# Windowed attention with block summaries, then a hard-swish MLP: every engine's queue in the order of the program, attention cut into parts by engine

## The chip, the cores and the metric

The kernel runs on one core of one Trainium2 chip. A core has a matrix engine (TensorE, PE in the profile), three engines for element-wise work (VectorE or DVE, ScalarE or ACT, GpSimd or POOL) and SyncE (SP), which here only issues transfers. Each engine works through a queue of its own, in order, and waits at semaphores for the others. The metric is device time in microseconds (us); less is better.

## The reference

Attention over 4 batches, 8 heads, 768 positions of 64 columns; then a two-layer MLP on the 3072 rows of 512 columns that the heads give together.

```python
k_sum = k.reshape(B, H, nb, block, D).max(axis=3)      # block = 32, nb = 24
v_sum = v.reshape(B, H, nb, block, D).mean(axis=3)
scores_l = scale * (q @ k^T), kept where abs(i - j) < 16
scores_s = scale * (q @ k_sum^T) + log(block)
a = softmax(concat(scores_l, scores_s))
x = (a @ concat(v, v_sum)), heads side by side         # 3072 x 512
h = x @ w_in                                           # 512 x 2048
out = (h * clip(h + 3, 0, 6) / 6) @ w_out              # 2048 x 512
```

## The kernel before

**Attention.** Heads go in four pairs p per batch b. For a query block of 64 positions the kernel forms one column block of 128 key rows: 64 own keys, 24 block maxima (rows 64 to 87), 16 keys after the block and 16 before it (the *edges*). `kx[p]` holds these for all 12 blocks, `qx[p]` the queries of both heads, `va[b % 2]` the values in the same row order, with weights for the denominator. Steps, with their lines:

- `Tk` (L241): 16 PE transposes of k into a PSUM tile `tpk`; ACT copies it into `kx` (L250); DVE takes the block maxima (L258), spreads them (L261), and copies the two edges from `tpk` (L271, L272).
- `Tq` (L274): transposes of q into `tpq`; ACT copies one head's half, DVE the other (L294; L296 for batch 3).
- `Sc` (L298): score matmuls for up to four blocks (L308), ACT's exponential into `at` (L310). In batches 0 and 1 the mask is added on PE (L304), in 2 and 3 DVE multiplies by it (L312).
- `AV` (L316): values times weights into `num`, denominators into `den`; ACT takes logarithm and exponential for the reciprocal (`lg`), DVE multiplies into `x` (L352; L337, L338 for batches 2 and 3). `num` and `den` have one buffer each.
- `v` of batches 0 and 1 is loaded as float32 (`vf`), cast into `va` by DVE and GpSimd (`cast_v`, L117), its block sums come from PE (`sum_v`, L389) and go into `va` through DVE (L391) and GpSimd (`put_sums`, L395). For batches 2 and 3 GpSimd sets the weights (12 memsets, L485), loads v straight into `va` (L127) and adds rows (`vsum`, L142).

**MLP.** 768 rows of a batch make two tiles of 384 rows, 8 tiles in all. `F1(t, ft)` (L356): four matmuls of 128x384 (L362) into `hp`, ACT's relu `r` (L365), DVE's product `g` (L366). `F2(t, i)` (L368): one matmul of 128x512 (L374); after 16 of them ACT copies the result `ot` and SP stores it. `hp` has two buffers, four where no F2 runs beside F1. `g` tiles and the two `vf` tiles share a pool of three.

**Order.** The work list (L526) is F1(0), F2(0), F1(1), F2(1), F1(2), then F1(t) with F2(t-1) for t = 3 to 7, then F2(7); each entry has 16 steps, here called *slots*, numbered 16n + i. A dictionary `plan` puts attention calls behind slots. But the program's order binds only GpSimd throughout; for PE, ACT, DVE and SP it binds up to L445 alone:

```python
    ctx.enter_context(tc.manual_schedule(engines={ET.Pool}))
    start = tc.manual_schedule(engines={ET.PE, ET.Activation, ET.DVE, ET.SP})
    start.__enter__()
    ...
    start.__exit__(None, None, None)
```

From there a scheduler, working at build time, picks each of these four queues' order from what the plan emits. A load issued by GpSimd waits until the transfer eight before it has landed, as the built program has eight semaphores for them.

Of the kernel before, what the change touches and what calls it, by code (L numbers as in the profile page):

```python
# [15 lines left out]
D = 64  # L16
# [16 lines left out]
def kernel(  # L33
# [39 lines left out]
    kx = [const.tile([128, NQ, 128], BF16, tag=f"kx{p}", name=f"kx{p}") for p in range(NP)]  # L73

    qx = [const.tile([128, NQ, 2, QB], BF16, tag=f"qx{p}", name=f"qx{p}") for p in range(NP)]
# [33 lines left out]
    def load_vf(b, p):  # L109

        t = vf_t[b][:, 2 * p:2 * p + 2].rearrange("r h s d -> r (h s) d")
        nc.gpsimd.dma_start(out=t, in_=v[b, 2 * p:2 * p + 2].rearrange("h s d -> (h s) d").rearrange("(s r) d -> r s d", r=128))

    def cast_v(eng, b, p, odd, lo, hi):

        t = vf_t[b][64 * odd:64 * odd + 64, 2 * p:2 * p + 2, lo:hi]
        eng.tensor_copy(va[b % 2][0:QB, p, 2 * lo + odd:2 * hi:2, 0:3:2].rearrange("r t j d -> r j t d"), t)  # L117
# [42 lines left out]
    start = tc.manual_schedule(engines={ET.PE, ET.Activation, ET.DVE, ET.SP})  # L160
    start.__enter__()
# [22 lines left out]
    q0 = rows_tile(ld_tile("qb"), 8, RUN // 2)  # L184
    load("k", 0, 0, 1, t=(k0, 0))
# [3 lines left out]
    load("q", 0, 0, 1, 0, t=(q0, 0))  # L189
    load_vf(0, 0)  # L190
    load_vf(0, 1)
# [13 lines left out]


    nc.vector.memset(zero[:], 0.0)
    nc.vector.memset(half_c[:], 0.5)

    nc.vector.memset(ind[:], 0.0)  # L210
    for u in range(4):
        nc.vector.memset(ind[32 * u:32 * u + 32, 28 + u:29 + u], 1.0)

    def zero_kq(p):
        nc.vector.memset(words(kx[p][:, :, R_SUM + NB:R_NEXT]), 0.0)
        nc.vector.memset(words(kx[p][:, 0, R_PREV:]), 0.0)
        nc.vector.memset(words(kx[p][:, NQ - 1, R_NEXT:R_PREV]), 0.0)
        for j in range(2):
            nc.vector.memset(words(qx[p][64 * j:64 * j + 64, :, 1 - j]), 0.0)

    for p in range(3):
        zero_kq(p)

    def zero_rest():
        nc.vector.tensor_scalar(mask[:], maskb[:], 1.0 / BIG, 1.0, op0=ALU.mult, op1=ALU.add)
        zero_kq(3)
        nc.vector.memset(ones[:, 1], 0.0)
        for i in (0, 2):
            nc.vector.memset(ones[:, i], 1.0)
            nc.vector.memset(ones[R_SUM:R_NEXT, i], float(BLK))  # L230

    def zero_va(i, p):
        z = zero[:].unsqueeze(2)
        nc.scalar.copy(words(va[i][:, p, :, 1]), z.to_broadcast([128, NQ, D // 2]))
        o = va[i][R_NEXT:, p, 0:NQ:NQ - 1].rearrange("r t j d -> r t (j d)").bitcast(F32)
        nc.scalar.copy(o, z[R_NEXT:].to_broadcast([32, 2, 3 * D // 2]))

    for p in range(NP):
        zero_va(0, p)

    def Tk(b, p):  # L241
        pool, tag = (ps_o, "o") if b == 0 else (ps_s, "s")
        tp = pool.tile([128, S], BF16, tag=tag, name="tpk")
        t = kq_t["k", b, p, None]
        o = kx[p][:, :, 0:QB]
        if b < NLONG:
            for s in range(RUN):
                for j in range(2):
                    nc.tensor.transpose(tp[64 * j:64 * j + 64, s * RP:(s + 1) * RP], t[:, j, s], ident[0:RP, 0:RP])  # L249
            nc.scalar.copy(o.rearrange("p t (c s) -> p t c s", s=RUN),  # L250
                           tp[:].rearrange("p (s t c) -> p t c s", s=RUN, t=NQ))
        else:
            for s in range(NT):
                nc.tensor.transpose(tp[:, s * 128:(s + 1) * 128], t[:, s].rearrange("p h d -> p (h d)"), ident[:])
            nc.scalar.copy(o, tp[:].rearrange("p (t c) -> p t c", t=NQ))
        red = work.tile([128, NB], BF16, tag="red", name="red")
# [4 lines left out]
        nc.vector.tensor_copy(kx[p][:, :, R_SUM:R_SUM + NB], red[:].unsqueeze(1).to_broadcast([128, NQ, NB]))  # L261
        if b < NLONG:
            e = EDGE // RUN
            src = tp[:].rearrange("p (s t c) -> p t c s", s=RUN, t=NQ)
            tail, head = src[:, 0:NQ - 1, RUN - e:], src[:, 1:, 0:e]
            put = lambda o: o.rearrange("p t (c s) -> p t c s", s=RUN)
        else:
            src = tp[:].rearrange("p (t c) -> p t c", t=NQ)
            tail, head = src[:, 0:NQ - 1, QB - EDGE:], src[:, 1:, 0:EDGE]
            put = lambda o: o  # L270
        nc.vector.tensor_copy(put(kx[p][:, 1:, R_PREV:]), tail)  # L271
        nc.vector.tensor_copy(put(kx[p][:, 0:NQ - 1, R_NEXT:R_PREV]), head)  # L272

    def Tq(b, p, half=None):  # L274
        pool, tag = (ps_h, "h") if b == 0 else (ps_s, "s")
        tp = pool.tile([128, S], BF16, tag=tag, name="tpq")
        t = kq_t["q", b, p, half]
        r = RUN if half is None else RUN // 2
        n = r * RP
        t0 = 0 if half is None else half * NH  # L280
        nt = n // QB
        if b < NLONG:
            for s in range(r):
# [5 lines left out]
        for j in range(2):  # L289
            rows = slice(64 * j, 64 * j + 64)  # L290
            copy = nc.vector.tensor_copy if j else nc.scalar.copy
            o = qx[p][rows, t0:t0 + nt, j]
            if b < NLONG:
                copy(o.rearrange("p t (c s) -> p t c s", s=r), tp[rows, 0:n].rearrange("p (s t c) -> p t c s", s=r, t=nt))  # L294
            else:
                copy(o, tp[rows].rearrange("p (t c) -> p t c", t=NQ))  # L296

    def Sc(b, p, lo, hi):  # L298
# [7 lines left out]
        for i in range(n):  # L306
            t = lo + i
            nc.tensor.matmul(sp[:, i], kx[p][:, t], qx[p][:, t], start=not on_pe, stop=not on_pe or i == n - 1)  # L308
        a = at[p][:, lo:hi]
        nc.scalar.activation(a, sp[:, 0:n], AF.Exp, scale=scl)  # L310
        if not on_pe:
            nc.vector.tensor_tensor(a, a, mask[:, m0:m0 + n].unsqueeze(2).to_broadcast([128, n, 2, QB]), op=ALU.mult)  # L312

    xt = {}

    def AV(b, p, half):  # L316
# [3 lines left out]
        a = at[p]  # L320
        alt = b == 0 and half == 0 and p % 2 == 1
        pool = ps_o if alt else ps_n
        num = pool.tile([128, HALF], F32, tag="o" if alt else "num", name="num")
        den = pool.tile([128, HALF], F32, tag="o" if alt else "den", name="den")
        lg = work.tile([128, HALF], F32, tag="lg", name="lg")
        if b in DEN_IN_VALUES:

            for j, o in enumerate((num, den)):
                for i in range(NH):
                    t = half * NH + i  # L330
                    w = va[b % 2][:, p, t].rearrange("p j d -> p (j d)")
                    nc.tensor.matmul(o[:, i * QB:(i + 1) * QB], w[:, j * D:j * D + 128], a[:, t, j],
                                     start=True, stop=True)
            nc.scalar.activation(lg[0:64], num[64:128], AF.Ln)
            nc.scalar.activation(lg[64:128], den[0:64], AF.Ln)  # L335
            nc.scalar.activation(lg[:], lg[:], AF.Exp, scale=-1.0)
            nc.vector.tensor_tensor(xt[s][0:64, p], num[0:64], lg[0:64], op=ALU.mult)  # L337
            nc.vector.tensor_tensor(xt[s][64:128, p], den[64:128], lg[64:128], op=ALU.mult)  # L338
            return
        for i in range(NH):  # L340
            t = half * NH + i
            w = va[b % 2][:, p, t].rearrange("p j d -> p (j d)")
            for j in range(2):
                nc.tensor.matmul(num[:, i * QB:(i + 1) * QB], w[:, j * D:j * D + 128], a[:, t, j],
                                 start=(i == 0 and j == 0), stop=(i == NH - 1 and j == 1))
        w = ones[:].rearrange("p j d -> p (j d)")
        for j in range(2):
            nc.tensor.matmul(den[:].rearrange("p (t c) -> p t c", c=QB), w[:, j * D:j * D + 128],
                             a[:, half * NH:(half + 1) * NH, j], start=(j == 0), stop=(j == 1))
        nc.scalar.activation(lg[:], den[:], AF.Ln)  # L350
        nc.scalar.activation(lg[:], lg[:], AF.Exp, scale=-1.0)  # L351
        nc.vector.tensor_tensor(xt[s][:, p], num[:], lg[:], op=ALU.mult)  # L352
# [31 lines left out]
    vs0 = [const.tile([R_NEXT, 2, D], BF16, tag=f"vs0{p}", name="vs0") for p in range(NP)]  # L384

    def sum_v(b, p):
        sums = ps_n.tile([128, 2, D], F32, tag=("num", "den")[p % 2], name="sums")
# [3 lines left out]
        nc.vector.tensor_copy(vs0[p][R_SUM:], sums[R_SUM:R_NEXT])  # L391
# [5 lines left out]

    def S_first(p):
        Sc(0, p, 0, 4)
        Sc(0, p, 4, 6)  # L400

    k1 = rows_tile(ld_tile("kb"), 4, RUN)

    def load_pair(p):
        load("k", 0, p, 1, t=(k1, 2 * p - 4) if p > 1 else (k0, 2 * p))
        load("q", 0, p, 1, 0, t=(q0, 2 * p))

    def v_first(p):
# [3 lines left out]
    load_pair(1)  # L412
    Tk(0, 0)
    Tq(0, 0, 0)
    zero_rest()
    cast_v(nc.gpsimd, 0, 0, 0, 0, 4)
    S_first(0)
    v_first(0)
    sum_v(0, 0)
    load_vf(0, 2)  # L420
    load_pair(2)
    put_sums(0, 0, 0, NH)
# [145 lines left out]
```

## Time and profile before

| | |
|---|---|
| median of two timed runs | 294.39 us (293.48 and 295.3) |
| the profiled execution | 293.38 us, span 291.7 us |
| busy: PE, DVE, ACT, POOL | 240.7, 158.8, 176.4, 113.7 us |
| mean granted TensorE clock | 0.958 |
| read from and written to HBM | 30.4 and 6.3 MB |

PE's busy time by stage, from the windows of the trace:

| stretch (us) | what runs | PE busy | clock |
|---|---|---|---|
| 0 to 40 | batch 0, first half | 22.06 of 40 | 0.96 |
| 40 to 71.3 | F1 of tile 0 | 11.14 of 31.3 | 0.67 |
| 71.3 to 128 | F2(0), F1(1), F2(1); attention of batches 0 and 1 | 55.63 of 56.7 | 1.00 |
| 128 to 153.5 | F1(2); end of batch 1, start of batch 2 | 21.94 of 25.5 | 1.00 |
| 153.5 to 235.4 | F1 and F2 together; batches 2 and 3 | 77.85 of 81.9 | 1.00 |
| 235.4 to 291.7 | F1 and F2, no attention | 52.05 of 56.3 | 0.99 |

How to read the profile: a line of the page's second part gives an engine's busy share in 40 equal slices of the span, as digits. A line of waits is "engine line waited for: us in total, times, longest". A timeline line is start, duration, engine, line, operation, output and input with shapes, count, and in brackets the idle time before it and what ended that. A window's line gives for each engine busy us and, in brackets, instructions.

### The profile page before, as it was taken

The page shows a single profiled execution, that of the slowest core. Times are in us where ns is not written, and L with a number is a line of the kernel's source. Part 1 is how long each engine was busy: PE and PEld are TensorE (multiplying, and loading weights), DVE is VectorE, ACT ScalarE, POOL GpSimd, SP SyncE. Part 2 cuts the span into 40 slices and gives each one's busy share as a digit, 9 for nine tenths or more (in the row PEclk, how much of TensorE's full clock was granted, in tenths as well). Part 3 has the DMA queues.
Part 4 walks back from the last instruction along what each step waited for, and adds up shares of the span by engine and source line. Part 5 has one row for each costly group of instructions (what it writes and reads, how often), then busy time and mean ns, then how long its engine had stood idle before and what let it go on. Part 6 is the DMA issues. An engine that isn't in the chain of part 4 may idle for free.

```text
span 291.7 us, 5339 instructions
## 1 busy us (share of the span) xinstructions
PE 240.7 (83%) x2035; PEld 140.8 (48%) x2060; DVE 158.8 (54%) x339; ACT 176.4 (60%) x337; POOL 113.7 (39%) x151
## 2 busy tenths in 40 slices
PE   1475782009999999999779999899999999999994
PEld 1254551004555765656545555555655555555541
DVE  4656540018335655529998567887685764443400
ACT  8422572005658555769776788977887865555421
POOL 7673496200010660599999999800000000000000
PEclk9999898557999999999999999999999999999999
DMA  5859499992042126499799979621000100100111
GB/s 105 162 100 139 73 200 190 206 231 60 2 75 108 19 39 110 84 291 154 82 83 130 202 161 127 93 62 39 36 3 36 38 36 36 38 37 36 38 72 72
DMA packets 45578, 27.75 MB, mean 95 GB/s; under 512 B 31216, under 2 KB 40816, under 8 KB 45168
## 3 DMA queue, kind: packets, MB, share of 16 engines
q0 software_dynamic: 36304, 18.35, 45.9%
q1 hardware_dynamic: 9248, 9.05, 11.9%
q8 instruction: 16, 0.26, 0.4%
q14 instruction: 10, 0.08, 0.1%
HBM read 30.41 MB, written 6.29 MB: 126 GB/s over the span
## 4 chain that ended last, share of the span: by engine, by line
PE 55%; ACT 15%; DVE 14%; DMA 6%; POOL 4%; issue 4%; ACTq 0%; POOLq 0%
PE op L374 21%; PE hp L362 19%; DMA vf<-in_v_dram 6%; PE sums L389 5%; ACT at L310 3%; DVE g L366 3%; ACT r L365 2%; PE sp L308 2%; DVE red L258 2%; DVE qx L294 2%; DVE at L312 2%; ACT lg L335 2%; DVE x L337 2%; PE sp L304 1%; DVE x L338 1%
## 5 line engine op out<-in xcount | busy, mean ns | idle before, releaser
L362 PE MATMUL hp<-x,win 128*128 128x384 bf16 x512 | 104.6, 330 | 26.4 <-DVE g L366 25.4
L365 ACT ACTIVATE r<-hp,half_c 128x384 f32<-128x384 f32 x128 | 73.6, 583 | 60.1 <-PE hp L362 34.9
L374 PE MATMUL op<-wout,g 128*128 128x512 bf16 x359 | 95.5, 379 | 1.5 <-issue 0.5
L366 DVE SCALAR_TENSOR_TENSOR g<-r,hp 128x384 bf16<-128x384 f32 x128 | 69.0, 552 | 43.9 <-ACT r L365 41.6
L362 PEld LDWEIGHTS <-win 128*128 128x128 bf16 x512 | 48.3, 99 | 65.4 <-issue 33.3
L374 PEld LDWEIGHTS <-g 128*128 128x128 bf16 x384 | 36.4, 98 | 32.6
L310 ACT ACTIVATE at<-sp 128x512 bf16<-128x512 f32 (+1 forms) x52 | 27.4, 563 | 16.9 <-PE sp L308 16.9
L308 PE MATMUL sp<-qx,kx 128*128 128x128 bf16 x192 | 18.5, 224 | 8.3 <-DVE qx L294 8.3
L395 POOL COPY va<-vs 32x768 bf16<-32x768 bf16 (+1 forms) x12 | 12.6, 1049 | 31.0 <-DVE vs L391 30.7
L308 PEld LDWEIGHTS <-kx 128*128 128x128 bf16 x192 | 14.8, 100 | 18.4 <-issue 8.9
L378 ACT COPY ot<-op 128x512 f32<-128x512 f32 x24 | 13.8, 584 | 10.6 <-PE op L374 10.4
L142 POOL TENSOR_TENSOR vr<-vr 96x1024 f32<-96x1024 f32 (+3 forms) x16 | 19.4, 1215 | 1.1
L258 DVE TENSOR_REDUCE red<-tpk 128x24 bf16<-128x768 bf16 x12 | 11.5, 955 | 15.4 <-ACT kx L250 15.4
L485 POOL MEMSET va<- 32x768 bf16 (+1 forms) x24 | 17.8, 740 | 1.0
L352 DVE TENSOR_TENSOR x<-num,lg 128x384 bf16<-128x384 f32 x16 | 8.9, 555 | 15.3 <-ACT lg L351 13.6
L117 DVE CAST va<-vf 64x384 bf16<-64x384 f32 (+1 forms) x12 | 5.3, 444 | 20.4 <-DMA vf<-in_v_dram 20.1
L250 ACT COPY kx<-tpk 128x768 bf16<-128x768 bf16 x12 | 9.7, 806 | 10.3 <-PE tpk L249 10.3
L99 POOL DMA_DIRECT2D qb<-in_q_dram x9 | 6.2, 685 | 24.4 <-PE tpq L285 24.3
L389 PE MATMUL sums<-vf,ind 128*32 128x128 f32 x96 | 14.7, 317 | 0.4 <-DVE x L352 0.4
L312 DVE TENSOR_TENSOR at<-at,mask 128x512 bf16<-128x512 bf16 x24 | 13.3, 569 | 2.1 <-ACT at L310 2.0
L294 DVE COPY qx<-tpq 64x384 bf16<-64x384 bf16 (+1 forms) x16 | 12.2, 760 | 3.9 <-ACT qx L294 3.5
L389 PEld LDWEIGHTS sums<-vf,ind 128*32 128x32 f32 x96 | 11.9, 130 | 3.2 <-issue 1.7
(69 smaller groups left out, 260.9 us busy)
## 6 DMA issues: line engine op xcount, KB each, us to landing
out_dram<-ot SPq DMA_DIRECT2D x24, 256.0 KB
vf<-in_v_dram POOLq DMA_DIRECT2D x8, 384.0 KB, 10.2
vr<-in_v_dram POOLq DMA_DIRECT2D x4, 768.0 KB, 8.9
win<-in_moe_w_in_dram POOLq DMA_DIRECT2D x4, 512.0 KB, 6.6
wout<-in_moe_w_out_dram POOLq DMA_DIRECT2D x4, 512.0 KB, 15.9
qb<-in_q_dram POOLq DMA_DIRECT2D x5, 384.0 KB, 6.4
kb<-in_k_dram POOLq DMA_DIRECT2D x4, 384.0 KB, 9.7
va<-in_v_dram POOLq DMA_DIRECT2D x16, 96.0 KB, 3.4
```

The lines of the kernel that those rows point to most:

```text
L142: nc.gpsimd.tensor_tensor(out=o, in0=r[:, 0:n], in1=r[:, n:2 * n], op=ALU.add)
L258: nc.vector.tensor_reduce(red[:], tp[:].rearrange("p (s n c) -> p n s c", s=RUN, n=NB), axis=AX.XY, op=ALU.max)
L294: copy(o.rearrange("p t (c s) -> p t c s", s=r), tp[rows, 0:n].rearrange("p (s t c) -> p t c s", s=r, t=nt))
L308: nc.tensor.matmul(sp[:, i], kx[p][:, t], qx[p][:, t], start=not on_pe, stop=not on_pe or i == n - 1)
L310: nc.scalar.activation(a, sp[:, 0:n], AF.Exp, scale=scl)
L312: nc.vector.tensor_tensor(a, a, mask[:, m0:m0 + n].unsqueeze(2).to_broadcast([128, n, 2, QB]), op=ALU.mult)
L362: nc.tensor.matmul(hp[:], w_in_sb[:, kt, ft * 128:(ft + 1) * 128], xt[t][:, kt], start=(kt == 0), stop=(kt == NP - 1))
L365: nc.scalar.activation(r[:], hp[:], AF.Relu, bias=half_c[:], scale=1.0 / 6.0)
L366: nc.vector.scalar_tensor_tensor(gt[t][:, ft], r[:], 1.0, hp[:], op0=ALU.min, op1=ALU.mult)
L374: nc.tensor.matmul(op[:], gt[t][:, ft, ts * 128:(ts + 1) * 128], w_out_sb[:, ft], start=(ft == 0), stop=(ft == NFT - 1))
L389: nc.tensor.matmul(sums[R_SUM:R_NEXT], ind[:, 28 - 4 * s:60 - 4 * s], vf_t[b][:, 2 * p:2 * p + 2, s], start=(s == 0), stop=(s == NT - 1))
L485: nc.gpsimd.memset(va[i][r0:r1, p, :, 1], float(w))
```

## The change

It does six things.

1. Program order binds PE, ACT, DVE and SP to the end, as it did GpSimd.
2. `Tk`, `Tq`, `Sc`, `AV` and `sum_v` are cut into parts by engine (`Tk_pe`, `Tk_act`, `Tk_dve`, `Tq_pe`, `Tq_out`, `Mk`, `AV_pe`, `AV_act`, `AV_dve`, `sum_pe`, `sum_dve`), and each part gets its own slot, with a lag of 1 or 2 slots between parts.
3. The edges of `kx` are no longer read from `tpk` by DVE but copied inside `kx` (`edges_k`): by ACT for batch 0, DVE for batch 1, GpSimd for batches 2 and 3. Both q halves of batch 1, and of batch 0, go to DVE; in batches 2 and 3 DVE comes first and ACT second.
4. GpSimd issues all first loads of batch 0 and half of `w_in` ahead of its own copies and casts; for pairs 0 and 1 the even casts go to ACT. q loads are joined in twos, v loads of batch 1 too.
5. Zeroing: `kx` and `qx` become one tile each and are cleared in few memsets; ACT clears the middle of `va[0]` in two copies (before: sixteen for both `va`), `va[1]` is cleared by GpSimd behind the first weights.
6. The casts and sums of batch 1's v get slots 33 to 40; `edges_v` of batches 2 and 3 comes after `vsum` on SP.

```diff
-    start = tc.manual_schedule(engines={ET.PE, ET.Activation, ET.DVE, ET.SP})
-    start.__enter__()
+    ctx.enter_context(tc.manual_schedule(engines={ET.PE, ET.Activation, ET.DVE, ET.SP}))
...
-    load("q", 0, 0, 1, 0, t=(q0, 0))
-    load_vf(0, 0)
-    load_vf(0, 1)
+    load("q", 0, 0, 2, 0, t=(q0, 0))
+    load_vf(0, 0, 1)
+    load("k", 0, 1, 1, t=(k0, 2))
...
+    load_vf(0, 1, 1)
+    load("k", 0, 2, 2, t=(k1, 0))
+    load("q", 0, 2, 2, 0, t=(q0, 4))
+    load_vf(0, 2, 1)
+    load_vf(0, 3, 1)
+    load_w_in(0)
+    load_w_in(1)
...
+    def edges_k(eng, p):
+        copy = eng.copy if eng is nc.scalar else eng.tensor_copy
+        copy(kx[:, p, 1:, R_PREV:], kx[:, p, 0:NQ - 1, QB - EDGE:QB])
+        copy(kx[:, p, 0:NQ - 1, R_NEXT:R_PREV], kx[:, p, 1:, 0:EDGE])
...
-        nc.vector.tensor_copy(put(kx[p][:, 1:, R_PREV:]), tail)
-        nc.vector.tensor_copy(put(kx[p][:, 0:NQ - 1, R_NEXT:R_PREV]), head)
...
+    k_in(0)
+    k_out(0)
+    S_first(0)
+    k_in(1)
+    cast_first(0, nc.scalar)
+    k_out(1)
+    sum_pe(0, 0)
+    sum_pe(0, 1)
...
+    def av(s, b, p, half, gap):
+        at_slot(s, AV_pe, b, p, half)
+        at_slot(s + 0.1, AV_act, b, p, half)
+        at_slot(s + gap, AV_dve, b, p, half)
...
     for p in range(NP):
-        at_slot(2 * p + 15, lambda p=p: Tq(0, p, 1))
-        at_slot(2 * p + 17, lambda p=p: (Sc(0, p, 6, 10), Sc(0, p, 10, 12)))
-        at_slot(2 * p + 21, lambda p=p: AV(0, p, 1))
...
+    for p in range(NP):
+        s = 33 + 2 * p
+        at_slot(s, sum_pe, 1, p)
+        at_slot(s + 1, sum_dve, p)
+        at_slot(s + 1, cast_v, nc.gpsimd, 1, p, 0, 0, 6)
+        at_slot(s + 1, cast_v, nc.vector, 1, p, 1, 0, 6)
+        at_slot(s + 1.5, put_sums, 1, p, 0, NQ)
+        at_slot(s + 1.5, edges_v, 1, p, p + 1, 0, NQ)
...
-        edges_v(b, 0, NP, 0, NQ)
         vsum(b, 0)
         vsum(b, 1)
+        edges_v(b, 0, NP, 0, NQ)
...
+    def attention(b, t_slots, av_slots, lag, sc):
+        eng = nc.vector if b == 1 else nc.gpsimd
         for p in range(NP):
+            s = t_slots[p]
+            at_slot(s, Tk_pe, b, p)
+            at_slot(s + 0.1, Tk_act, b, p)
+            at_slot(s + lag, Tk_dve, b, p)
+            at_slot(s + lag, edges_k, eng, p)
+            at_slot(s + lag, Tq_pe, b, p)
+            at_slot(s + lag + 0.1, Tq_out, b, p, 1, nc.vector.tensor_copy)
+            at_slot(s + lag + 0.1, Tq_out, b, p, 0, nc.scalar.copy if b > 1 else nc.vector.tensor_copy)
+            s += sc
+            for i in range(3):
+                at_slot(s + i * lag / 2, Sc, b, p, 4 * i, 4 * i + 4)
+                at_slot(s + i * lag / 2 + lag, Mk, b, p, 4 * i, 4 * i + 4)
...
-    for b, s0, s1 in ((2, 48, 56), (3, 71, 81)):
+    for b, s0, s1 in ((2, 48, 56), (3, 72, 82)):
...
-    attention(1, 42, 4, lambda i: (56, 58, 61, 63, 65, 68, 71, 74)[i])
+    attention(1, (40, 44, 48, 51), (52, 54, 57, 60, 65, 68, 71, 74), 2, 4)
     for b in range(2, B):
         base = 64 + 32 * (b - 2)
-        order = (14, 16, 24, 26, 18, 20, 28, 30)
-        attention(b, base, 5, lambda i, base=base: base + order[i])
+        attention(b, [base + 5 * p for p in range(NP)], [base + i for i in (14, 16, 24, 26, 18, 20, 28, 30)], 1, 4)
```

For batches 2 and 3 the call at slot s1 (56, 82) emits, for GpSimd, the second k and q loads, the loads of v for the sums, 12 memsets, eight loads of v and ten additions, and only behind these, in its queue, come `edges_k` of the same batch's first pair (slots 65 and 97).

## The prediction

> **What bounds the kernel now.** I read the page first: tenths by slice, with PE at 0 in the middle.
>
> ```profile
> PE   1475782009999999999779999899999999999994
> DVE  4656540018335655529998567887685764443400
> ACT  8422572005658555769776788977887865555421
> POOL 7673496200010660599999999800000000000000
> ```
>
> PE is the bound nearly everywhere from 70 us on; the losses are the first 40 us (about 18 us idle, from the windows by ten) and the hole in slices 6 to 8. The waits name the hole, the timeline shows its cause:
>
> ```profile
> DVE va L117 <- DMA vf<-in_v_dram: 20.1, 1, 20.1
> PE hp L362 <- DVE g L366: 25.4, 13, 19.9
> DVE qx L294 <- ACT qx L294: 3.5, 3, 1.8
> ```
> ```profile
> 40.92 3.27 DVE L366 SCALAR_TENSOR_TENSOR g<-r,hp 128x384 bf16<-128x384 f32 x6 [1.03 <-ACT r L365]
> 41.53 4.06 PE L362 MATMUL hp<-x,win 128*128 128x384 bf16 x24 [0.28 <-DVE g L366]
> ...
> 64.27 0.56 DVE L117 CAST va<-vf 64x768 bf16<-64x768 f32 x1 [20.07 <-DMA vf<-in_v_dram]
> ...
> 65.46 5.88 PE L362 MATMUL hp<-x,win 128*128 128x384 bf16 x24 [19.87 <-DVE g L366]
> ```
>
> After six g's of the first tile the scheduler put batch 1's v cast into DVE's queue; it waits for a load issued at 46.17, and all g's stand behind it. Next I asked for the windows between points that I can find in both programs:
>
> ```profile
> 71.30:88.40 17.10, 16.84 (x165) 9.79 (x168) 6.13 (x11) 9.66 (x23) 1.51 (x2) 1.00 0.20 33
> 88.40:120.20 31.80, 31.26 (x321) 19.95 (x321) 17.56 (x35) 20.38 (x36) 10.09 (x10) 1.00 0.32 72
> 135.00:153.50 18.50, 14.99 (x194) 9.54 (x192) 18.38 (x35) 14.79 (x30) 17.70 (x20) 1.00 1.08 94
> 153.50:235.40 81.90, 77.85 (x637) 44.51 (x649) 58.53 (x120) 66.91 (x129) 34.52 (x43) 1.00 0.62 82
> 235.40:291.70 56.30, 52.05 (x269) 26.50 (x271) 19.30 (x35) 24.48 (x44) 0.00 (x0) 0.99 0.12 47
> ```
>
> (columns: busy PE, weight loads, DVE, ACT, POOL, then clock and DMA). Only 135 to 153.5 is bound by another engine, DVE. Last, GpSimd's queue:
>
> ```profile
> 119.75 0.67 POOL L99 DMA_DIRECT2D kb<-in_k_dram  x1 [9.91 <-PE tpk L249]
> 120.50 0.67 POOL L99 DMA_DIRECT2D qb<-in_q_dram  x1
> 121.17 1.05 POOL L131 DMA_DIRECT2D vr<-in_v_dram  x2
> 122.26 9.28 POOL L485 MEMSET va<- 64x768 bf16 x12
> 131.49 5.99 POOL L127 DMA_DIRECT2D va<-in_v_dram  x8
> 137.54 5.09 POOL L142 TENSOR_TENSOR vr<-vr 96x1024 f32<-96x1024 f32 x4
> ...
> 148.23 0.38 POOL L142 TENSOR_TENSOR vs<-vr 96x64 bf16<-96x64 f32 x1
> ```
>
> From batch 1's last q transposes (done at 120.2) to the end of batch 2's v sums at 148.6 it takes 28.4 us; nobody waits for that now.
>
> **The change, part by part.** I carry a clock through both programs, with one "slot" for each ft of the work list. The profiled execution takes 293.38 us, its span 291.7, so 1.7 lie around it; the median of the two timed runs is 294.39, 0.3% more. The order of the built program gives the queues; all durations are the trace's.
>
> *Start (x of tile 0: 39.95 before).* ACT's 16 zeroings of va end at 8.60 and only then ACT copies the first k (8.62), although its transposes ended at 5.63. Two larger copies (0.51 us for 384 columns, so about 0.95 each) end near 4. k copy 5.7 to 6.5; DVE maximum 0.96, spread 0.55, two q copies of 0.56: first scores at 9.3 instead of 12.23. Then 24 float32 sums at the cold rate of 5.07 us, after pair 1's transposes, end near 16.7; pairs 2 and 3 each cost DVE 2.2 us behind ACT's k copy (0.8) and edges (two, by the 0.34 of the 32x192 copy), to 21.0 and 23.9. The last two AVs share one num and one den: each 0.9 PE + 1.05 ACT + 0.56 DVE + handing over, 2.7 us. x complete at 31.8. Below, 28 if waits overlap; above, 36 with loads late: the 2.75 MB of k, q and v move in 17 us at the 162 GB/s of the best early slice, in 25 at its worst of 105.
>
> *Stall out.* The casts of batch 1 move to slots 34 to 40. F1 of tile 0 is 64 x 0.165 (36 in 5.93) plus a ramp of 0.7, 11.3; F2 of tile 0 with batch 0's second half 17.1 as the window above. F1 of tile 1 starts at 31.8 + 11.3 + 17.1 = 60.2, before 88.3: **-28.1**. What is late next is v of batch 1, now for the sums on PE at slot 33, near 61. GpSimd issues it after zeroing va1 (about 2.4 us by the 0.74 of a 768-column memset) instead of ACT. All loads up to it are about 10.1 MB (7.3 for batch 0 and the weights, 1.2 of k and q, 1.6 of v); with early slices near 150 GB/s and later ones at 200 its halves land near 55 and 59. If not, PE itself waits, and everything in order behind it.
>
> *Slots 32 to 53, to batch 1's last q transposes.* PE work: F1 10.5, 18 F2 x 0.215 = 3.9, 4 sums x 1.43, 8 transposed groups x 0.47, 8 score parts x 0.44, one AV 0.67: 28. For batch 1 both q copies and both edges now are DVE's: 0.95 + 0.2 + 0.5 + 2 x 0.95 = 3.6 us between transposes and scores that stand two slots (1.3 us) later; for two of the pairs g of the same slot is ahead too. Waits of 3.0 and 2.0, then near nothing: 33.2, against 31.8. **+1.4** (0 to +4). The point is reached at 93.4.
>
> *The edges of batches 2 and 3 on GpSimd.* They stand behind the v sums in the rows above. Before, scores of batch 2 began 14.8 us after the last q transposes (135.0). Now GpSimd needs 28.4 from there, plus two copies (0.6). None is in the trace: between L142's 0.35 for 64 columns of two inputs and L395's 0.84 for 768 of one, I take 0.3 each for 176 columns (0.2 to 0.6). PE's own way to these scores is about 21 us: 30 F2 (6.5), 20 F1 (3.3), four AVs (2.7), scores and transposes (2.7), and some 6 of waits for the AV chain (PE 0.67, ACT 1.0, DVE 0.56) behind q copies. So PE, in program order, stands some 8 us at batch 2's first scores, with all of F1 behind: **+14.2** (12 to 16), scores at 122.4. Batch 3's same wait: GpSimd needs 5.2 + 1 + 9.5 + 6 + 10.9 + 0.6 = 33 from the transposes of slot 80, PE 31.5 (20 slots of 1.30, seven AVs of 0.6, 1.3 of scores and transposes) without and 36 with other waits: 0 to 2, taken 0. On SP the v edges now follow the copies of the sums, and tile 2's three outputs stand behind both; ACT's fourth output copy (slot 101, three buffers) may wait some 2 us for them, which the hp buffers cover (0 to 2).
>
> Here the clock is a rule to weigh. In the trace the 24 matmuls after the 19.9 us hole took 5.88 us against 4.06 for the 24 before it, with a granted clock of 0.50 in the hole. TensorE: Matmul & The Clock Gate (section "What's actually happening") says an idle window of about 3.4 us is enough to throttle to half; by it the new 8 us hole costs an estimated 1.7 us again. I take none, as the slots that follow are not PE's to bound; the range has it.
>
> *Slots 68 to 80.* Whoever reads a PSUM tile second waits for the first reader (the third wait above). q's two halves were ACT, then DVE; now DVE is first, behind g, maximum and spread: 0.55 + 0.95 + 0.2 + 0.95 = 2.65 us in which ACT can't go on to its next relu. Then DVE waits for ACT's 0.79 + 0.58. DVE loses six edge copies (1.8 of 18.4) and the masks that took 2.26 instead of 0.42 beside GpSimd's sums, but two engines now take turns three times: 16.6 + 3 x (0.8 + 0.79 + 0.58) = 23.1, against 18.5. **+4.6** (0 to +7).
>
> In the trace one of batch 2's mask multiplications took 2.26 us, the median of nine 0.42, while GpSimd added rows. SBUF — State Buffer (section "SBUF: two separate sides") names the cause: the port pair that DVE and GpSimd share is locked for a whole instruction, also by a DVE operation with two inputs in SBUF. By it an edge copy on GpSimd could hold up a mask, an estimated 0.3 us each time; no run shows that yet, and the sum goes without it.
>
> *Slots 80 to 128.* PE works 77.85 of 81.9. The hand-over now meets two hp buffers, not four: relu, g, maximum, spread, copy, copy, relu, g take 4.7 us from one F1 to the free buffer, PE's work in between 3.6: 1.1 us for three pairs, 2 where an AV shares the slot (two pairs): **+7.3** (0, if PE's queue has other work, to 5 x 3.5 = 17.5).
>
> *The rest* (56.3) has no attention and stays. Merged memsets, v loads in two, kx as one tile lie beside waiting engines: nothing, under 1 us if not.
>
> Sum: span 291.7 - 28.1 + 1.4 + 14.2 + 4.6 + 7.3 = 291.1, time 292.8.
>
> **The rivals.**
> A, faster: the hand-overs are hidden, as DVE and ACT have a third of their time free between 153.5 and 235.4; GpSimd's wait stays. 292.8 - 1.4 - 4.6 - 7.3 = 279.5; with a slower start 285. For it, the free time; against, each engine now takes its work in order.
> B, slower: ACT's q copy behind DVE's, in slots 80 to 116. Price 3.5 us for each of five pairs rather than 7.3 in all: +10.2, 303. It decides from 3 us a pair (292.8 + 5 x 3 - 7.3 = 300.5). For it, an AV's logarithms, too, stand behind that copy; against, the slack above.
> C, the stall only changes engine: v of batch 1 as late as before (64.2 to about 70) holds the sums of slots 33 to 39 by 3 to 5 us: 297.
>
> **How the numbers follow.** About 2%, 288.5 to 300.3 around 294.39, is what a measurement here can tell from no change. Forecast 0.35 and C 0.08 lie within it; A 0.33 is faster, B 0.24 slower. I say 292.8. Within "the same" alone the time would be 289 to 299; since A and B hold over half, the range runs from 278 (A with a start at 30) to 305 (B with one cold restart).
>
> **What would show it.** Right: no wait of DVE for v; F1 of tile 1 near 60; one wait of PE at line 317 for GpSimd's edges of some 8 us near 115 to 122; ACT waiting at line 303 for DVE; PE fuller in the first 32 us. Wrong: PE at line 407 waiting for the load; first scores of batch 2 before 115; slots 80 to 128 in under 83 us (A) or over 95 (B).

## The result, and the profile after

The changed kernel takes 318.75 us (318.69 and 318.8) against 294.39: 1.083 times the time before, 95% interval 1.068 to 1.097. The prediction said 292.8, range 278 to 305. The profiled execution has a span of 317.1 us, 25.4 more than before.

The page of the changed kernel, in tenths by slice (a slice is now 7.9 us), with the granted TensorE clock below:

```profile
PE   2874879999677981759649898867849899999995
DVE  6564684247677142175564656336545555444410
ACT  5454753555445661554848675545767675555521
POOL 7827960129103999470199991000000000000000
PEclk9999999999799996596998999979978999999999
```

The hole of slices 6 to 8 is gone. In its place PE has a deep one in slice 15, beside a GpSimd at 9, and unbroken 9s come only from slice 32. The clock, which was 9 from slice 10 on before, is below that in seven of the slices 15 to 30. The waits name what PE, ACT and DVE lack (the columns: who, line, waited for whom; us in total, times, longest):

```profile
DVE g L382 <- ACT r L381: 106.0, 79, 11.5
...
ACT qx L303 <- DVE qx L303: 12.4, 4, 3.9
...
ACT qx L305 <- DVE qx L305: 10.9, 4, 3.1
...
PE num L339 <- DVE x L368: 10.0, 7, 3.0
PE num L339 <- DVE x L365: 8.7, 2, 4.4
...
PE sp L317 <- POOL kx L271: 7.9, 1, 7.9
...
PE sp L317 <- DVE qx L303: 4.6, 3, 2.1
...
ACT ot L394 <- DMA out_dram<-ot: 1.6, 1, 1.6
```

No DVE wait for v is left. New are ScalarE's eight waits for VectorE's copy of q (23.3 us together), PE's one wait for GpSimd's edges, and PE's waits for x, that is for the multiplication that frees num and den. Now the clock that the prediction carried, in us from the span's start:

| point | before | predicted | after |
|---|---|---|---|
| first tile's F1 running | 39.95 | 31.8 | 33.64 |
| F1 of tile 1 | 88.3 | 60.2 | 64.13 |
| last q transposes of batch 1 done | 120.2 | 93.4 | 100.5 |
| first scores of batch 2 (slot 68) | 135.0 | 122.4 | 129.16 |
| slot 80 | 153.5 | 145.5 | 155.92 |
| slot 128 | 235.4 | 234.7 | 261.22 |
| end of span | 291.7 | 291.1 | 317.1 |

Up to slot 68 the change is still 5.8 us ahead. Slots 68 to 128 then take 132.1 us, before 100.4. The windows between those points in the changed kernel (busy PE, weight loads, DVE, ACT, POOL, then clock, DMA share, GB/s):

```profile
64.13:100.00 35.87, 31.04 (x297) 18.94 (x297) 23.16 (x46) 18.26 (x33) 11.86 (x10) 0.95 0.34 63
100.00:129.16 29.16, 16.75 (x188) 9.79 (x189) 9.17 (x15) 12.54 (x24) 27.11 (x35) 0.86 0.85 119
129.16:155.92 26.76, 19.64 (x201) 12.42 (x201) 13.16 (x26) 16.77 (x33) 7.81 (x12) 0.77 0.75 76
155.92:261.22 105.30, 83.43 (x632) 46.95 (x641) 56.56 (x111) 66.64 (x127) 35.51 (x50) 0.94 0.41 59
261.22:317.10 55.88, 51.87 (x268) 26.51 (x271) 19.30 (x35) 24.31 (x43) 0.00 (x0) 0.99 0.13 48
```

In the third and fourth rows PE is busy 103.1 us, in the same stretch of before 14.99 + 77.85 = 92.8 at clock 1.00. So of the 31.7 us lost there, 10.2 are about as many matmuls (833 records, 831 before) at a lower clock, 0.77 and 0.94, and 21.4 are idle PE. No engine is full there. DVE is busy 53% of the time and ACT 63%, before 77% and 81%: they wait for one another. One such place, from the timeline of all engines:

```profile
160.40 0.96 DVE L303 COPY qx<-tpq 64x768 bf16<-64x768 bf16 x1
161.39 0.79 ACT L303 COPY qx<-tpq 64x768 bf16<-64x768 bf16 x1 [3.86 <-DVE qx L303]
162.21 0.49 ACT L352 ACTIVATE lg<-num 64x384 f32<-64x384 f32 x1
162.72 0.48 ACT L353 ACTIVATE lg<-den 64x384 f32<-64x384 f32 x1
163.24 0.52 ACT L356 ACTIVATE lg<-lg 128x384 f32<-128x384 f32 x1
163.67 1.04 ACT L381 ACTIVATE r<-hp,half_c 128x384 f32<-128x384 f32 x2
164.26 0.56 DVE L382 SCALAR_TENSOR_TENSOR g<-r,hp 128x384 bf16<-128x384 f32 x1 [2.90 <-ACT r L381]
164.74 0.54 DVE L365 TENSOR_TENSOR x<-num,lg 64x384 bf16<-64x384 f32 x1
...
165.34 0.35 PE L339 MATMUL num<-at,va 128*128 128x64 bf16 x6 [4.43 <-DVE x L365]
```

ScalarE has nothing to do for 3.86 us because its half of q is read after VectorE's. Behind that copy in its queue stand the logarithms of an AV and two relus; VectorE's next g waits 2.90 us for the first relu, the multiplication that frees num stands behind that g, and PE, with the next AV first in its queue and F1 behind it, waits 4.43 us.

### The profile page after: what moved, and what is told of

Its sections match the earlier page's. It is cut to its first block, busy times and chain, and to the rows that moved or that the text cites. A ratio compares the mean times of both kernels' runs of the same rounds, so it can differ in the third digit from the quotient of the medians.

```text
span 317.1 us, 5297 instructions
## 1 busy us (share of the span) xinstructions
PE 249.5 (79%) x2035; PEld 144.2 (45%) x2060; DVE 157.6 (50%) x315; ACT 172.0 (54%) x321; POOL 117.8 (37%) x162
## 4 chain that ended last, share of the span: by engine, by line
PE 42%; DVE 24%; ACT 13%; POOL 8%; issue 6%; DMA 5%; SPq 0%; ACTq 0%; POOLq 0%
PE op L390 16%; PE hp L378 15%; DVE g L382 7%; ACT r L381 4%; DVE qx L303 3%; DMA va<-va 3%; PE sp L317 3%; POOL vr L144 3%; POOL va L532 3%; DVE x L366 2%; DVE red L277 2%; POOL va L129 2%; DMA out_dram<-ot 2%; PE sums L407 2%; DVE x L365 2%
## 5 line engine op out<-in xcount | busy, mean ns | idle before, releaser
L378 PE MATMUL hp<-x,win 128*128 128x384 bf16 x512 | 106.4, 341 | 8.9 <-DVE g L382 7.6
L390 PE MATMUL op<-wout,g 128*128 128x512 bf16 x359 | 97.6, 385 | 3.4 <-DVE g L382 1.8
L317 PE MATMUL sp<-qx,kx 128*128 128x128 bf16 x192 | 20.5, 240 | 15.3 <-POOL kx L271 7.9
L339 PE MATMUL num<-at,va 128*128 128x64 bf16 x288 | 14.1, 196 | 23.1 <-DVE x L368 10.0
L339 PEld LDWEIGHTS <-va 128*128 128x128 bf16 x384 | 15.5, 100 | 33.9 <-DVE x L365 11.9
L317 PEld LDWEIGHTS <-kx 128*128 128x128 bf16 x192 | 16.5, 109 | 25.6 <-issue 10.9
L303 DVE COPY qx<-tpq 64x384 bf16<-64x384 bf16 (+1 forms) x28 | 20.3, 727 | 7.4 <-PE tpq L289 7.1
L270 POOL COPY kx<-kx 128x176 bf16<-128x176 bf16 x8 | 2.7, 332 | 54.8 <-ACT kx L266 34.6
L415 POOL COPY va<-vs 32x768 bf16<-32x768 bf16 (+1 forms) x12 | 14.3, 1190 | 19.5 <-DVE vs L411 18.9
L144 POOL TENSOR_TENSOR vr<-vr 96x1024 f32<-96x1024 f32 (+3 forms) x16 | 19.1, 1194 | 1.1
L356 ACT ACTIVATE lg<-lg 128x384 f32<-128x384 f32 x32 | 16.7, 522 | 1.0
L355 ACT ACTIVATE lg<-den 128x384 f32<-128x384 f32 x16 | 7.8, 490 | 11.6 <-PE den L344 11.4
```

Source lines behind the costliest of these rows:

```text
L144: nc.gpsimd.tensor_tensor(out=o, in0=r[:, 0:n], in1=r[:, n:2 * n], op=ALU.add)
L317: nc.tensor.matmul(sp[:, i], kx[:, p, t], qx[:, p, t], start=not on_pe, stop=not on_pe or i == n - 1)
L339: nc.tensor.matmul((num, den)[j * both][:, i * QB:(i + 1) * QB], w[:, j * D:j * D + 128], a[:, t, j], start=both or (i == 0 and j == 0), s ...
L378: nc.tensor.matmul(hp[:], w_in_sb[:, kt, ft * 128:(ft + 1) * 128], xt[t][:, kt], start=(kt == 0), stop=(kt == NP - 1))
L390: nc.tensor.matmul(op[:], gt[t][:, ft, ts * 128:(ts + 1) * 128], w_out_sb[:, ft], start=(ft == 0), stop=(ft == NFT - 1))
```

## The experiments

Two theories came first. Theory 1: ScalarE held by VectorE's copy does most of the harm. Rival 2: the fixed order as such does, whatever the order of the copies. A second question was what the wait for GpSimd is worth. The first four runs were made together; each is compared with the kernel before on its own chip (there 296.86 us in the median of seven).

**ScalarE first.** The order of two lines; only the dependence between the copies turns round:

```
-            at_slot(s + lag + 0.1, Tq_out, b, p, 1, nc.vector.tensor_copy)
             at_slot(s + lag + 0.1, Tq_out, b, p, 0, nc.scalar.copy if b > 1 else nc.vector.tensor_copy)
+            at_slot(s + lag + 0.1, Tq_out, b, p, 1, nc.vector.tensor_copy)
```

> Batches 2 and 3 copy q's first half on ScalarE before VectorE copies the second; all else as in the changed kernel. Theory 1 (ScalarE held): the 8 waits of ScalarE for VectorE's q copy (12.4 + 10.9 = 23.3 us) are what holds relu and the logarithms, and with them PE; they go, the two PE holes of 4.4 and 4.3 us before AV go, and slots 68 to 128 shrink from 132 us to 110 to 118: 297 to 305 us. Rival 2 (the fixed order itself): two hp buffers and one num/den pair bind in any order of the copies, VectorE now waits for ScalarE instead: less than 7 us gained, 312 to 318 us.

Measured 306.19 us (303.96 to 307.18), 1.038 (1.027 to 1.050): 12.6 less, between the theories. ScalarE's eight waits are gone, so are PE's holes of 4.4 and 4.3, and slots 68 to 128 take 118.3 us (128.0 to the end of the span less the 55.9 of the rest). But a new hole came up, in the timeline of this run:

```profile
189.01 0.65 SPq L125 DMA_DIRECT2D va<-va  x1
189.72 0.63 SPq L126 DMA_DIRECT2D va<-va  x1
190.44 6.74 SPq L396 DMA_DIRECT2D out_dram<-ot  x4
...
196.24 0.58 ACT L394 COPY ot<-op 128x512 f32<-128x512 f32 x1 [7.20 <-DMA out_dram<-ot]
...
197.37 0.80 PE L292 MATMUL tpq<-ident,qb 128*128 128x128 bf16 x6 [6.55 <-ACT at L319]
```

SyncE issues the outputs only behind the copies of the v sums and the value edges. ScalarE's fourth output copy finds all three buffers taken and waits 7.20 us, PE behind it 6.55. In the changed kernel the same wait was 1.6, because ScalarE came late to it: SyncE issued the outputs there at 196.90 and ScalarE reached the copy at 201.16; here the times are 190.44 and 189.04. In both the buffer came free 5.8 us after the issue.

**Edges on VectorE.**

```
-        eng = nc.vector if b == 1 else nc.gpsimd
+        eng = nc.vector
```

> The key edges of batches 2 and 3 are copied by VectorE, as in batch 1, not by GpSimd. If GpSimd's queue is what the first scores of batch 2 wait for, PE's wait of 7.9 us at line 317 falls below 1.5, these scores start near 122, and the matmuls after them run at the full clock: 310 to 313 us. VectorE has 0.43 us more for each of eight pairs, at most 3.4 in all. Rival: something else of the queue (v sums, value loads) is as late, and the wait goes to the first AVs of batch 2: less than 3 us gained, 316 to 319 us.

Measured 312.25 us (311.27 to 313.32), 1.060 (1.050 to 1.071): 6.5 less. The interval overlaps a little with the changed kernel's 1.068 to 1.097, so the size is less sure than the trace: PE's wait at line 317 is gone, and the scores start at 122.6, 6.6 us earlier. The rest of the 7.9 us is with the AV just ahead of them, which waits 3.58 us for x (3.03 in the changed kernel). The clock was not restored as expected: the eight scores still take 1.06 us, as they did after the wait for GpSimd (1.03).

**The scheduler again, from the first slot, and from slot 64.** The fixed order of the four engines ends at that point, the parts, slots, start and GpSimd's queue stay:

```
-    ctx.enter_context(tc.manual_schedule(engines={ET.PE, ET.Activation, ET.DVE, ET.SP}))
+    order = tc.manual_schedule(engines={ET.PE, ET.Activation, ET.DVE, ET.SP}); order.__enter__()
...
-        for i in range(NFT):
+        for i in (order.__exit__(None, None, None) if n == 4 else None) or range(NFT):
```

(the second hunk for slot 64; for the first slot the order ends on the line of `plan = {}`)

> The fixed program order of TensorE, ScalarE, VectorE and SyncE ends where the slots begin; from there the scheduler orders them, as in the kernel before. The parts, their slots, the new start and GpSimd's queue stay. In the order so built 11 of the first tile's 16 g stand ahead of the first two casts of batch 1's v (six before). Theory 1 (the dependence between the two q copies does the harm, in whatever order): slots 68 to 128 keep half of their loss, and part of the stall for v returns (0 to 10 us): 300 to 312 us. Rival 2 (the fixed order does it): slots 68 to 128 as before the change, about 100 us: 285 to 298 us.

> As the run before it, but the fixed order ends only at slot 64, so that the start and the whole of tiles 0 and 1 stay as in the changed kernel (slot 64 at 112.2 us) and no cast can be put ahead. Theory 1: the scheduler moves relus ahead of ScalarE's q copy, yet the copies stay chained: half of the 31 us come back, 300 to 308 us. Rival 2: all of it comes back, and GpSimd's wait is filled with F1 of tile 2: 286 to 296 us.

Measured 280.52 (279.83 to 281.23), 0.952 (0.943 to 0.962), and 278.63 (276.31 to 280.22), 0.943 (0.929 to 0.957). Theory 1 falls as the main cause: with nothing changed but the end of the fixed order, the time falls by 40 us, so what the order costs after slot 64 is more than either theory had. The windows and PE's timeline of the run that ends the order at slot 64:

```profile
130.00:150.00 20.00, 18.27 (x197) 10.68 (x198) 15.70 (x28) 14.75 (x27) 11.83 (x22) 1.00 1.04 117
150.00:170.00 20.00, 18.27 (x155) 9.98 (x157) 12.30 (x24) 16.08 (x31) 19.57 (x27) 1.00 1.29 163
```
```profile
126.94 4.06 PE L378 MATMUL hp<-x,win 128*128 128x384 bf16 x24
130.84 0.81 PE L390 MATMUL op<-wout,g 128*128 128x512 bf16 x2
131.48 0.49 PE L378 MATMUL hp<-x,win 128*128 128x384 bf16 x2
132.65 0.56 PE L317 MATMUL sp<-qx,kx 128*128 128x128 bf16 x7 [0.68 <-POOL kx L271]
```

Here the first scores of batch 2 run at 132.65, 3.5 us *later* than in the changed kernel, the edges are still GpSimd's, and it costs 0.68 us: F1 of tile 2 and the first F2 of the next stage have been pulled ahead of them, and the attention parts slide to slots where PE has work of its own. PE is busy 18.27 of 20 us at clock 1.00. ScalarE's waits for the q copies shrank from 12.4 to 2.1 us in batch 2, although VectorE still copies first.

**Both edits, and the outputs first**, in the fixed order (kernel before 293.4 here):

> Both single edits at once, in the fixed order: ScalarE copies q's first half before VectorE, and VectorE copies the key edges. If the two waits add (318.75 less 12.6 and 6.5): 298 to 302 us. Rival: with these waits gone the output copies, which wait for three outputs behind the v sums and edges on SyncE (one wait of 7.2 us in the run with ScalarE first, 1.6 in the changed kernel), take the place of one of them: 303 to 307 us.

300.36 us (297.95 to 303.19), 1.024 (1.014 to 1.033): the two add (12.6 + 6.5 = 19.1, measured 18.4), though the output wait stayed at 5.5 us. Then, as well:

```
-        vsum(b, 0)
-        vsum(b, 1)
         edges_v(b, 0, NP, 0, NQ)
+        vsum(b, 0)
+        vsum(b, 1)
```

> As the run before it, and the value edges are issued ahead of the v sums on SyncE, as in the kernel before the change. If SyncE's order holds the outputs: ScalarE's wait of 7.2 us at the output copy goes, and the time falls by 5 to 7 us against the run before it (292 to 297 us). Rival: the eight row copies of the sums hold the outputs, not the two edges behind them: less than 2 us.

294.83 us (291.75 to 296.17), 1.006 (1.001 to 1.010): 5.5 less, and the output wait is gone. It was not the moment of the issue that decided, though: SyncE issued these outputs at the same time in both runs, 184.27 us and now 184.22. What no longer stands just ahead of them is the two transfers of the value edges, 264 KB each. With them there, the first output freed its buffer 5.8 us after its issue (ScalarE's copy started at 190.09). Without them ScalarE came to the copy 2.4 us after the issue, at 186.58, and did not wait. With its three large waits gone the fixed order only equals the kernel before, which has a 20 us stall that it has not.

**The stall alone**, in the kernel before, one word:

```
-        cast_v(nc.vector, 1, p, 1, 0, 6)
+        cast_v(nc.gpsimd, 1, p, 1, 0, 6)
```

> The kernel before the change, with one word changed: GpSimd, not VectorE, makes the odd-row casts of batch 1's v, so that no g of the first tile stands behind that load. This prices the stall by itself, under the scheduler. If the stall is worth its 19.9 us: 273 to 279 us. Rival: the same load holds something else next (the sums on PE, or VectorE's copy of them, in queues the scheduler fills early): less than 10 us gained, 285 us or more.

271.76 us (269.5 to 272.58), 0.927 (0.918 to 0.937): 21.6 less, the stall's 19.9 and 1.7 more, the size of the cold clock behind it (5.88 us instead of 4.06 for 24 matmuls); this is the fastest kernel of the study. GpSimd now waits for the load 6.2 us, and nobody waits for GpSimd's casts. Its page:

```profile
PE   2294769999999999977999999999999999999994
...
PEclk9999799999999999999999999999999999999999
```

**Where the order may end.** From slot 48, beside 277 to 280 for slot 64:

> The fixed order holds to slot 48 rather than 64, then the scheduler. If the fixed order still costs its waits in the slots 48 to 64 (in the run that ended it at 64, PE was idle 6.0 of the 30 us from 80 to 110, most of it before scores of batch 1): 3 to 5 us less than that run, 273 to 276 us. Rival: these waits belong to batch 1's parts (both q copies and both edges on VectorE) in any order: no difference, 277 to 280 us.

277.33 us (275.28 to 278.65), 0.947 (0.939 to 0.955): no difference, the rival.

Then the start's own worth, on the scheduler from slot 32 (casts on GpSimd as above), with and without the three edits:

> The changed kernel's start and parts; fixed order only to slot 32, then the scheduler; the three edits of the fixed-order runs (ScalarE first, edges on VectorE, value edges ahead of the sums) and GpSimd for the odd casts of batch 1. If the earlier start (x at 33.6 instead of 39.95 us) and the stall's removal add: about 6 us less than the 271.8 of the kernel before with the casts moved, 263 to 268 us. Rival: the later loads set when batch 1 can go on, and the earlier start only waits for them: 270 to 276 us.

> The same without the three edits: q's copies VectorE first, edges on GpSimd, value edges behind the sums. If the scheduler covers these waits with other work, as PE's 0.68 us at batch 2's first scores in the run with the order ended at slot 64 suggests: within 2 us of the run before it. Rival: they cost under the scheduler too (24 us in the fixed order): 6 us or more above it.

275.14 (271.51 to 276.79), 0.933 (0.919 to 0.947), and 273.64 (272.28 to 274.17), 0.934 (0.927 to 0.942). The three edits, worth 24 us in the fixed order, are worth nothing under the scheduler. And the earlier start gains nothing over 271.76: x is there at 33.6 instead of 39.9, but the second tile's F1 follows F2 at 65.6 instead of 66.4. In between, F1 of the first tile takes 12.7 us instead of 9.5 (granted clock 0.89 instead of 1.00), and F2 with the second half of batch 0's attention 19.3 instead of 17.0 (these numbers are from the run with the three edits, 275.14).

**Distances**, on the fixed order with the three edits. Two slots instead of one between the parts of batches 2 and 3 (`lag` 2 for 1 in the call of `attention`):

> The fixed order with the three edits, and the distance between a part and the next (transposes to copies, scores to masks, AV to x) two slots instead of one in batches 2 and 3. Theory (the distance of one slot, 1.3 us, is shorter than the hand-over through three engines, so PE meets each result before it is there): PE's waits for x (some 15 us there) halve, 285 to 291 us. Rival (any hand-written order pays, whatever the distance, since one num/den pair serves all AVs): 293 to 298 us.

311.36 us (307.61 to 312.1), 1.062 (1.050 to 1.074), worse by 16.5: both were wrong. Two lines of its waits grew, from 3.3 and 9.9 us in the run before the edit:

```profile
PE num L339 <- DVE x L365: 17.3, 12, 3.4
...
PE num L339 <- DVE x L368: 11.4, 6, 6.2
```

The first line is the edit. Line 365 serves batches 2 and 3: the multiplication that frees num and den now stands two slots down VectorE's queue, and PE stands in its own queue until then, 14.0 us longer in all. Line 368 serves batches 0 and 1, whose distances the edit leaves alone, so 9.9 of the 15 us in the theory were out of its reach. That line's longest wait, 6.18 us, has something else in it: two copies of VectorE ahead of that multiplication took 2.24 and 1.27 us while GpSimd added rows of v (their medians in this run are 0.24 and 0.20).

So the reverse was tried, half a slot:

```
-            av(av_slots[i], b, p, half, lag)
+            av(av_slots[i], b, p, half, lag if b == 1 else 0.5)
```

> The fixed order with the three edits; in batches 2 and 3 the multiplication that frees num and den stands in VectorE's queue in the same slot as its AV (half a slot on), ahead of the next slot's g, instead of behind it. Theory (the place of that multiplication sets how long PE waits for num and den; two slots of distance made it worse by 16.5 us): PE's waits for x fall from 15 to 8 us or less, 286 to 291 us. Rival: VectorE then stands waiting for the logarithms with g behind it, and PE waits for hp instead: 294 to 302 us.

293.25 us (290.77 to 295.08), 0.999 (0.994 to 1.004): 1.6 less, but the intervals overlap, so a gain is not shown. PE's wait at line 365 fell from 3.3 to 1.5 us, its waits for g rose from 5.3 to 7.4. One is traded for the other, and again the 9.9 us at line 368 (now 9.5) were out of reach.

Last, the four odd casts of batch 0 behind the 16 g of the first tile, on the scheduler from slot 32 (`at_slot(15, ...)` for `at_slot(2 + 3 * p, ...)`, its edges too):

> As the run with the order fixed to slot 32 and no other edits, with the four odd casts of batch 0's second half behind all 16 g of the first tile, not among them. If these casts (0.35 us, but 0.80 and 1.25 beside GpSimd's work in that run) are why F1 of the first tile takes 12.7 us after the earlier start against 9.5 in the kernel before with its casts moved: 2 to 3 us less, 270 to 272 us. Rival: GpSimd-side work and the clock hold it, or the casts then hold the AVs of the second half: within 1 us, or slower.

Four times from 271.69 to 279.41, at granted clocks from 1.00 to 0.97; the spread is larger than the 2 to 3 us in question. So it stays open whether those casts or the clock lengthen F1 after the earlier start; why F2 takes longer, too, was not tried.

## Why the prediction was wrong, step by step

- *Start*: 33.64 against 31.8; two AVs waited 3.1 us for value edges, which the sum had not. (In its upper end, 2.75 MB at 105 GB/s are 26 us, not 25.)
- *Stall out*: as predicted, DVE's wait is gone and nothing took its place (rival C falls: PE's sums never waited for the load). F1 took its 11.3; F2 19.2 instead of 17.1, for a cause that was not taken apart. -24.2 of -28.1. That the stall was worth its length is shown by the one-word run.
- *Slots 32 to 53*: 36.4 instead of 33.2, just past the +4 of its upper end. PE waits for VectorE's q copies, as worked out: it is idle 4.8 us, where the sum had 5.0. What was too small is PE's own work, 31.5 us instead of 28, in part because the clock fell to 0.81 from 79 to 88 us.
- *Edges on GpSimd*: scores 28.7 us after the last q transposes (29.0 predicted), wait 7.88 (8 predicted). Right, as a step of this order. What was left out is that the price exists only in this order: under the scheduler it is 0.68 us.
- *Outputs behind the v sums*, taken at 0 with at most 2: 1.6 here, but 7.2 as soon as ScalarE was quicker, and 5.5 us of the time in the run that moved the value edges from in front of them.
- *Clock*, taken at nothing: 10.2 us in slots 68 to 128. The prediction counted one hole. In the trace the granted clock was 0.63 and 0.50 in the 4.7 us behind the holes of 4.43 and 4.28 us, and it fell after shorter holes too (last section). The Trainium skill, TensorE: Matmul & The Clock Gate (section "What's actually happening"), speaks of an idle window of about 3.4 us. The step failed in counting holes by the one wait it had priced.
- *Slots 68 to 80*: +8.3, against +4.6 and an upper end of +7.
- *Slots 80 to 128*: **the step that failed**: +23.4, against +7.3 and an upper end of 17.5. The mechanism stood in the text (ScalarE held by VectorE's q copy; rival B at 3.5 us a pair), and the two largest holes of this stretch, 4.43 and 4.28 us, have it. The mistake was in what stands behind the held engine. The sum followed relu, g and two hp buffers to PE, 1.1 us a pair, 2 with an AV. That path measured about what it was given: PE's waits for g are 7.6 us, 1.9 before. The trace shows a second ring, for which the sum had only the 0.9 us more of two pairs: ScalarE's logarithms, VectorE's multiplication, the single num and den, PE's next AV, with all of F1 and F2 behind it in program order. PE's waits for that multiplication are 10.4 us, 0.2 before. The lower clock adds 5.6 (PE busy 83.4 instead of 77.9). These three make 21 of the 23.4; the rest is mostly waits of PE for ScalarE. With ScalarE's copy put first the two holes shrink to 1.55 and 1.40 us, so it is shown that the held copy makes them. Slots 68 to 128 then still take 118.3 us, before 100.4; the run that ends the fixed order at slot 64 wins this back as well.
- *Rest*: 55.9, against 56.3.

The misses add up: 3.9 to tile 1, 3.2 in slots 32 to 53, -0.3 at the edges, 3.7, 16.1, -0.4; together 26.2, where the span is 26.0 longer than predicted (the rest is rounding).

Behind the steps lies one thing that the prediction never priced. It took the stretches of before (18.5, 81.9) as the kernel's own and added hand-overs. They were the scheduler's: it had let F1 and F2 pass any part that was not ready. That "each engine now takes its work in order" was set down as an argument against rival A and given no number. (The argument for A misread its row: of the 81.9 us VectorE was free for 29% and ScalarE for 18%, not a third.) The fixed order with its three large waits removed (294.83) and the same parts under the scheduler from slot 32, with batch 1's odd casts on GpSimd (275.14), differ by some 20 us. The part of that which lies in slots 68 to 80 is shown in the windows of the former (25.0 us, with the clock at 0.86); which of the many small waits make up the rest was not taken apart further, and the two runs on distances say only that moving the multiplication of batches 2 and 3 trades waits.

## What to carry to other kernels

When a change takes the order away from a scheduler, price every hand-over as if nothing could pass it, and follow the held engine's whole queue, not only the next instruction: here the wait that ended on PE was two engines further on. When one instruction stalls a queue, move that instruction first: here one word gave 21.6 us of what the rewrite was after, and the rewrite lost 24. A wait that is removed in a fixed order can hand the place to the next (the outputs' 1.6 us became 7.2), so edits are tried together before any is judged. And a buffer that waits for a transfer waits for what is queued ahead of that transfer: two copies in front of the outputs cost 5.5 us, though the outputs were issued no earlier without them.

## What the runs showed of the hardware

The granted clock dropped after holes shorter than the 3.4 us window named above. Two of them, of 2.06 and 2.50 us, in PE's timeline of the changed kernel:

```profile
82.82 0.38 PE L317 MATMUL sp<-qx,kx 128*128 128x128 bf16 x4 [2.06 <-DVE qx L303]
...
83.60 1.44 PE L378 MATMUL hp<-x,win 128*128 128x384 bf16 x4
...
206.26 0.81 PE L390 MATMUL op<-wout,g 128*128 128x512 bf16 x3
209.57 1.10 PE L378 MATMUL hp<-x,win 128*128 128x384 bf16 x4 [2.50 <-DVE g L382]
210.46 1.49 PE L390 MATMUL op<-wout,g 128*128 128x512 bf16 x3
```

Four F1 matmuls take 1.44 us instead of 0.81 behind the first, three F2 matmuls 1.49 instead of 0.81 behind the second, with a granted clock of 0.62 from 209.5 to 214. After a hole of 1.93 us, at 221.16, four F1 took their 0.81. What decides between 1.93 and 2.06 us was not tried.

VectorE beside GpSimd: in the run with the multiplication half a slot on, two masks while GpSimd adds v rows, and two later ones:

```profile
125.41 3.45 DVE L325 TENSOR_TENSOR at<-at,mask 128x512 bf16<-128x512 bf16 x2
...
135.15 0.76 DVE L325 TENSOR_TENSOR at<-at,mask 128x512 bf16<-128x512 bf16 x2
```

The Trainium skill, SBUF — State Buffer (section "SBUF: two separate sides"), describes a lock of the port pair that the two share, for a VectorE operation with two inputs in SBUF against a GpSimd operation that reads there; these rows agree with it. The earlier the scores of batch 2 come, the more of their masks meet the v sums: the longest mask took 0.60 us with these scores at 129.2 (the changed kernel), 1.28 at 122.6 (edges on VectorE) and 2.07 at 121.7 (the value edges first as well). The prediction's estimate that GpSimd's edge copies could hold up a mask by 0.3 us each came true once: of 24 masks of the changed kernel one took 0.60 us instead of 0.42, at 228.01, where an edge copy ran (228.01 to 228.34). Copies with one input can be slow there, too: in the run with two slots a copy of 128x288 took 2.24 us at 121.59, while GpSimd added rows, and 0.24 in the median. A cast of 64x384 with one input took 0.35 us at 38.45 and 1.34 at 42.48, while GpSimd issued the loads of batch 1's v (42.21 to 45.09); whether the issue is the cause was not tried.
